# Loading x on one DMA queue, ordering weight loads behind scratch writes, and moving a conversion forward in an engine's order: a Fourier-mixing and MLP kernel on one core

## The chip, the cores and the metric

The kernel runs on one core of one Trainium2 chip. The metric is the device time of one execution in microseconds (us). Each kernel was executed several times, on the same chip as runs of the kernel before, and the medians are given with their range.

The engines go by their names in the profile: PE is TensorE, DVE is VectorE, ACT is ScalarE, POOL is GpSimd, SP is SyncE, and an added q (SPq, POOLq) means the engine's sequencer, which also issues DMAs. In the text I call them TensorE, Vector, Scalar, GpSimd and SyncE.

## The reference

```python
# x: (8, 3008, 256) float32; w_in: (256, 2048) float64; w_out: (2048, 256) float64
X = np.fft.fft(x, axis=1)
X = np.fft.fft(X, axis=2)
x = X.real.astype(np.float32).reshape(24064, 256)
h = x @ w_in
g = h * np.clip(h + 3.0, 0.0, 6.0) / 6.0
return (g @ w_out).astype(np.float32)
```

The weights arrive as 64-bit floats. The kernel computes in float32, so they are loaded in 16 pieces of 512 KB as pairs of 32-bit words and converted to float32 with bit operations. "Conversion" below means this.

## The kernel before

The batches are worked in pairs. For the first pair nothing is there to overlap with, and the kernel begins with a start phase of some 118 us that runs as follows.

1. Eight *chunks* of x are loaded. Each has a direct load (`xt`) and a mirrored one (`xr`), a gather through a list of row numbers `IX`. The two are *folded* (added) on GpSimd, then on Vector.
2. Stage 1 of the Fourier transform multiplies the folded chunk on TensorE. Scalar copies the result out of PSUM as `z`, which I call an *eviction*, and a DMA writes `z` to a scratch in DRAM.
3. When all eight chunks are written, the scratch is read back transposed (`g`), stage 2 runs, and the first matmul of the MLP (`u`) can start.
4. In between, the first weight pieces are converted and folded into the transform (`wps`, `wns`), or mixed (`G`) for w_out.

The order of the program is the order of each engine. That is why it matters where a conversion stands.

```python
def load_x(pr, c):
    xt, xr = x_tile(pr, 2 * c), x_tile(pr, 2 * c + 1)
    nr, eng = (PR + 2, nc.sync) if pr.p == 0 else (PR, nc.gpsimd)    # PR = 94
    rows = x_pn[pr.p * PR:pr.p * PR + nr]
    n = XC if c < NXC - 1 else XC - 1
    eng.dma_start(out=xt[0:nr, 0:n, :], in_=rows[:, c * XC + 1:c * XC + 1 + n, :])
    ...
    nc.gpsimd.indirect_dma_start(                                    # the gather, 94 rows
        out=xr[0:PR].rearrange("p n d -> p (n d)"), out_offset=None, in_=x_r,
        in_offset=bass.IndirectOffsetOnAxis(ap=IX[:, i:i + 1], axis=0))

def stage1(pr, c, i):
    ...
    nc.scalar.copy(z[:, 2 * i:2 * i + 2, :], ps[0:PZ])               # eviction
    if i == XC // 2 - 1:
        (nc.scalar if pr.p == 0 else nc.sync).dma_start(out=..., in_=z[:])   # scratch write

def narrow_a(j):          # Vector: bits; Scalar: three ACTIVATEs for the exponent
    ...
def narrow_b(j):
    st, hi, ex, frac = raw.pop(j)
    nc.vector.scalar_tensor_tensor(ex[:], hi, -2 ** 31, ex[:], op0=AL.bitwise_and, op1=AL.bitwise_or)
    o = st[:].bitcast(F32)[:, 0:WB]
    nc.gpsimd.tensor_tensor(o, frac, ex[:].bitcast(F32), op=AL.mult)
...
load_x(first, 0); load_w(0); load_w(1)
nc.sync.dma_start(out=C[:], in_=...)
load_x(first, 1); load_x(first, 2)
...
narrow_pair(0); use_pair(0)                    # pieces 0 and 1
for c in range(NXC):                           # eight chunks
    fold(first, c, 0, nc.gpsimd)
    fold(first, c, 1, nc.vector)
    if c + 3 < NXC: load_x(first, c + 3)
    if c < 6: load_w(c + 2)
    if c == 5: load_t(0)
    for i in range(XC // 2): stage1(first, c, i)
    if c in (2, 5):                            # pieces 2, 3 (w_in), then 4, 5 (w_out)
        narrow_pair((c + 1) // 3); use_pair((c + 1) // 3)
load_w(8); load_w(9)
load_g(first, 0); load_g(first, 1)             # the read-back
```

## Time and profile before

| | before |
|---|---|
| time, median of 4 (range) | 2093.55 us (2093.17 to 2095.99) |
| span of the profiled execution | 2090.5 us |
| TensorE busy | 1978.4 us, 95% of the span |
| first fold of x starts | 30.55 us |
| last eviction of the start phase ends | 99.65 + 0.58 = 100.23 us |
| read-back issued | 103.39 us |
| stage 2 starts | 108.38 us |
| first `u` matmul starts | 117.73 us |

The last five rows are times in the trace, counted from the start of the span. TensorE is the bound of the whole, but the start phase is a chain of waits. So the first `u` matmul is the mark that I follow. The lines of the profile are in the prediction. There L153 is the first add of a fold, L410 the multiply of a conversion, L195 stage 1, L196 the eviction, L223 stage 2 and L268 the MLP's first layer. The changed kernel is two lines shorter above them, so its numbers are two lower, or one lower from L410 on.

### The profile page before, as it was taken

Reading aid. Unit: us, or ns where it says so; the run is one execution under the profiler, and the core shown is the slowest. Engines: PE = TensorE matmul, PEld = TensorE weight load, DVE = VectorE, ACT = ScalarE, POOL = GpSimd, SP = SyncE. Lnnn points to the kernel's source line nnn. Section 1 sums busy time; section 2 is a strip of 40 time slices with the busy share of each in tenths; the row PEclk is TensorE's granted clock in tenths of the full one; section 3 lists DMA queues with packets and bytes.
Section 4 is the critical chain, followed back from the end, with each engine's and each line's share of the span. In section 5 each row is a group of like instructions: output and inputs, shape, how many; then the busy total and the mean of one; then the engine's idle time right before and its main releaser. Section 6 shows DMA issues by size and latency. Waiting matters only on the chain.

```text
span 2090.5 us, 28142 instructions
## 1 busy us (share of the span) xinstructions
PE 1978.4 (95%) x9136; PEld 1692.8 (81%) x9136; DVE 1455.1 (70%) x2707; ACT 706.7 (34%) x1205; POOL 1499.2 (72%) x1660
## 2 busy tenths in 40 slices
PE   3467999999999999999999999999999999999997
PEld 1246888888888888888888888888888888888886
DVE  4446766777677677767677677677677777777775
ACT  2334333333333333333333333333333333333332
POOL 4437878788677788788667788787866766766765
PEclk7578999999999999999999999999999999999999
DMA  7330221111111112112101111221120011011000
GB/s 200 94 101 21 54 56 42 43 41 45 28 24 31 43 35 60 49 41 50 33 21 32 45 34 43 44 51 48 24 45 11 14 25 21 16 25 21 16 16 18
DMA packets 158272, 86.87 MB, mean 42 GB/s; under 512 B 132496, under 2 KB 145136, under 8 KB 158128
## 3 DMA queue, kind: packets, MB, share of 16 engines
q1 hardware_dynamic: 129968, 60.28, 12.8%
q0 software_dynamic: 27264, 21.65, 3.9%
q10 hardware_dynamic: 896, 3.15, 0.5%
q8 instruction: 74, 1.21, 0.3%
q14 instruction: 70, 0.57, 0.1%
HBM read 47.71 MB, written 37.22 MB: 41 GB/s over the span
## 4 chain that ended last, share of the span: by engine, by line
PE 89%; DVE 3%; ACT 1%; issue 1%; POOL 1%; DMA 0%; SPq 0%; DVEq 0%; POOLq 0%; ACTq 0%
PE acc L322 53%; PE v L268 16%; PE u L268 15%; PE ps L195 2%; PE ps L223 2%; PE ps L239 1%; DVE a L300 1%; ACT t L297 1%; PE wps L447 0%; DVE u L281 0%; DVE s L273 0%; DVE o L348 0%; POOL st L410 0%; DVE v L287 0%; PE ps L192 0%
## 5 line engine op out<-in xcount | busy, mean ns | idle before, releaser
L312 POOL TENSOR_TENSOR c<-a 128x512 f32<-128x512 f32 (+1 forms) x384 | 478.6, 1246 | 408.4 <-DVE a L300 243.2
L322 PE MATMUL acc<-c,G 128*128 128x256 f32 (+1 forms) x3072 | 712.5, 375 | 0.0
L322 PEld LDWEIGHTS acc<-c,G 128*128 128x128 f32 x3072 | 578.5, 190 | 73.3
L297 ACT ACTIVATE t<-u,half 128x512 f32<-128x512 f32 (+2 forms) x416 | 272.2, 654 | 1074.4 <-DVE u L281 1062.8
L273 DVE SCALAR_TENSOR_TENSOR s<-qn,WN,u 128x256 f32<-128x256 f32 x768 | 334.8, 478 | 386.9 <-PE u L268 386.9
L322 PE MATMUL acc<-a,G 128*128 128x256 f32 (+1 forms) x2304 | 554.8, 377 | 0.0
L322 PEld LDWEIGHTS acc<-a,G 128*128 128x128 f32 x2304 | 437.7, 192 | 57.7
L268 PE MATMUL v<-q,W 128*128 128x256 f32 x1536 | 399.3, 383 | 17.9 <-DVE a L300 17.9
L268 PE MATMUL u<-q,W 128*128 128x256 f32 x1536 | 394.5, 379 | 0.0
L268 PEld LDWEIGHTS v<-q,W 128*128 128x128 f32 x1536 | 291.4, 191 | 64.3 <-issue 21.6
L268 PEld LDWEIGHTS u<-q,W 128*128 128x128 f32 x1536 | 287.4, 190 | 65.2 <-issue 20.4
L300 DVE SCALAR_TENSOR_TENSOR a<-t,u 128x512 f32<-128x512 f32 (+2 forms) x416 | 266.2, 646 | 104.8 <-ACT t L297 99.9
L312 POOL TENSOR_TENSOR c<-a,c 128x256 f32<-128x256 f32 (+1 forms) x384 | 274.6, 715 | 30.1
L312 POOL TENSOR_TENSOR c<-c,a 128x256 f32<-128x256 f32 (+1 forms) x384 | 274.5, 715 | 30.1
L281 DVE TENSOR_TENSOR u<-s,v 128x512 f32<-128x512 f32 (+1 forms) x384 | 263.0, 685 | 43.0 <-PE v L268 3.0
L297 ACT ACTIVATE t<-v,half 128x512 f32<-128x512 f32 (+1 forms) x384 | 257.0, 669 | 6.2 <-DVE v L287 4.8
L287 DVE TENSOR_TENSOR v<-v,s 128x512 f32<-128x512 f32 (+1 forms) x384 | 257.9, 672 | 1.1
L300 DVE SCALAR_TENSOR_TENSOR a<-t,v 128x512 f32<-128x512 f32 (+1 forms) x416 | 255.3, 620 | 0.7 <-ACT t L297 0.4
L195 PE MATMUL ps<-y,F 94*96 94x512 f32 x120 | 72.0, 703 | 41.4 <-DVE y L161 35.3
L312 POOL TENSOR_TENSOR r<-w,e 128x256 f32<-128x256 f32 (+1 forms) x96 | 92.2, 981 | 3.8
L328 ACT ACTIVATE e<-acc 128x512 f32<-128x512 f32 (+1 forms) x192 | 86.9, 543 | 2.9 <-PE acc L322 2.8
L348 DVE STREAM_TRANSPOSE o<-r 128x256 f32<-128x256 f32 (+1 forms) x192 | 72.5, 416 | 6.5 <-POOL r L312 6.4
(69 smaller groups left out, 826.4 us busy)
## 6 DMA issues: line engine op xcount, KB each, us to landing
out_dram<-o SPq DMA_DIRECT2D x736, 32.0 KB
g<-zd SPq DMA_DIRECT2D x48, 256.0 KB
zd<-z SPq DMA_DIRECT2D x24, 384.0 KB
xt<-in_x_dram POOLq DMA_DIRECT2D x21, 376.0 KB, 3.9
st<-in_moe_w_in_dram SPq DMA_DIRECT2D x8, 512.0 KB
st<-in_moe_w_out_dram SPq DMA_DIRECT2D x8, 512.0 KB
zd<-z ACTq DMA_DIRECT2D x8, 384.0 KB
xt<-in_x_dram SPq DMA_DIRECT2D x7, 384.0 KB
```

The source lines that it names most:

```text
L195: nc.tensor.matmul(ps[0:PZ], F[0:PR, 0:PZ], y[:, 2 * i:2 * i + 2, :], start=True, stop=True)
L223: nc.tensor.matmul(ps[:, blk, 2 * u:2 * u + 2], g[:, kk, blk * P:(blk + 1) * P], T[:, :, gr, blk, kk], start=True, stop=True)
L268: nc.tensor.matmul(ps[:, i], W1[:, blk, f * P:(f + 1) * P], q[:, blk, of:of + KC], start=True, stop=True)
L273: nc.vector.scalar_tensor_tensor(s[:, i].rearrange("p k n -> p (k n)"), qn[:, of * N2:(of + KC) * N2], WN[:, f:f + 1], u[:, i].rearrange(" ...
L281: nc.vector.tensor_tensor(u[:, :, 0:ns], s[:, :, 0:ns], v[:, :, 0:ns], op=AL.add)
L287: nc.vector.tensor_tensor(v[:, :, 0:nm], v[:, :, 0:nm], s[:, :, 0:nm], op=AL.subtract)
L297: nc.scalar.activation(t, h, AF.Relu, bias=half[:], scale=scale)
L300: nc.vector.scalar_tensor_tensor(dst, t, 1.0, h, op0=AL.min, op1=AL.mult)
L312: nc.gpsimd.tensor_tensor(out, in0, in1, op=AL.add)
L322: nc.tensor.matmul(ch.acc[i // 2][:, i % 2, 0:ch.n], G[:, i, fc, :], mv, start=(fc == 0 and i % 2 == 0), stop=(fc == NF - 1), skip_group_c ...
L328: nc.scalar.mul(ch.e[:, k:i + 1, 0:ch.n], ch.acc[i // 2][:, 0:i + 1 - k, 0:ch.n], 1.0 / WS)
L348: nc.vector.transpose(o[:, 0:n // DH, h], ch.r[:, m, h, 0:n].rearrange("p (j i) -> p j i", i=DH))
```

## The change

Three things are changed in the start phase. All direct loads of x go to GpSimd's queue, with 94 rows instead of 96, so that SyncE's queue has only weights, tables and scratch traffic. Each weight piece from 2 on is issued on SyncE behind a scratch write, which also moves to SyncE, so that pieces no longer crowd the first loads of x: I call this *gating*. And the conversion of pieces 2 to 5 comes ahead of stage 1 of chunks 2 and 5, so ahead of those evictions in Scalar's order, and the multiply of pieces 0 to 5 moves to Vector: I call this *the order*.

```diff
 def load_x(pr, c):
-    nr, eng = (PR + 2, nc.sync) if pr.p == 0 else (PR, nc.gpsimd)
-    rows = x_pn[pr.p * PR:pr.p * PR + nr]
+    rows = x_pn[pr.p * PR:(pr.p + 1) * PR]
-    eng.dma_start(out=xt[0:nr, 0:n, :], in_=...)
+    nc.gpsimd.dma_start(out=xt[:, 0:n, :], in_=...)
 ...
-            (nc.scalar if pr.p == 0 else nc.sync).dma_start(      # scratch write
+            nc.sync.dma_start(
 ...
-        nc.gpsimd.tensor_tensor(o, frac, ex[:].bitcast(F32), op=AL.mult)
+        eng = nc.vector if j < 6 else nc.gpsimd
+        eng.tensor_tensor(o, frac, ex[:].bitcast(F32), op=AL.mult)
 ...
-    load_x(first, 0)
-    load_w(0)
-    load_w(1)
+    for j in range(2):
+        load_w(j)
     nc.sync.dma_start(out=C[:], ...)
-    load_x(first, 1)
-    load_x(first, 2)
+    for c in range(3):
+        load_x(first, c)
 ...
     for c in range(NXC):
 ...
-        if c < 6:
-            load_w(c + 2)
-        if c == 5:
-            load_t(0)
+        if c in (2, 5):
+            narrow_pair((c + 1) // 3)
         for i in range(XC // 2):
             stage1(first, c, i)
+        for j in {0: (2, 3), 2: (4,), 3: (5,), 5: (6,), 6: (7,), 7: (8, 9)}.get(c, ()):
+            load_w(j)
+        if c == 4:
+            load_t(0)
         if c in (2, 5):
-            narrow_pair((c + 1) // 3)
             use_pair((c + 1) // 3)
-    load_w(8)
-    load_w(9)
     load_g(first, 0)
```

(The tile of x shrinks to 94 rows, and a memset moves from GpSimd to Vector.)

## The prediction

> **What bounds the kernel now.** I read the page first, for where TensorE is not yet full. Its 40 slices are 52 us each:
>
> ```profile
> PE   3467999999999999999999999999999999999997
> PEclk7578999999999999999999999999999999999999
> ...
> PE 89%; DVE 3%; ACT 1%; issue 1%; POOL 1%; DMA 0%; SPq 0%; DVEq 0%; POOLq 0%; ACTq 0%
> ```
>
> From the fifth slice on (about 200 us) TensorE is at 90% or more, and the chain that ended last is 89% TensorE. The change touches nothing there. What it can win lies in the first four slices. The stretches of 20 us (columns: stretch, length, busy us with instruction counts for PE, PEld, DVE, ACT, POOL; granted clock, DMA share, GB/s) say how they are filled:
>
> ```profile
> 20.00:40.00 20.00, 6.79 (x24) 3.22 (x22) 3.02 (x6) 2.20 (x5) 7.99 (x6) 0.65 0.73 183
> 80.00:100.00 20.00, 7.96 (x16) 3.92 (x16) 8.71 (x19) 4.89 (x10) 9.81 (x10) 0.50 0.16 47
> ...
> 180.00:200.00 20.00, 14.61 (x63) 12.33 (x62) 13.39 (x23) 8.65 (x15) 15.05 (x18) 0.83 0.00 1
> 200.00:220.00 20.00, 20.00 (x91) 16.80 (x89) 15.04 (x28) 7.73 (x14) 16.75 (x19) 1.00 0.18 39
> ```
>
> No engine is full before 200 us: this is a chain of waits. So I followed it in order of time (start, length, engine, line, what; in brackets the idle time before it and what ended it):
>
> ```profile
> 4.03 1.70 POOL L141 DMA_INDIRECT xt<-in_x_dram,IX  x1 [3.58 <-DVE IX L465]
> 30.55 1.25 POOL L153 TENSOR_TENSOR xt<-xt 94x508 f32<-94x508 f32 x1 [12.83 <-DMA xt<-in_x_dram,IX]
> 51.08 0.72 ACT L398 ACTIVATE ex<-ex,bias 128x512 f32<-128x512 int32 x1 [0.44 <-ACT z L196]
> 54.12 1.27 POOL L410 TENSOR_TENSOR st<-top,ex 128x512 f32<-128x512 f32 x1 [9.34 <-DVE ex L408]
> 80.00 1.26 POOL L410 TENSOR_TENSOR st<-top,ex 128x512 f32<-128x512 f32 x1 [11.39 <-DVE ex L408]
> 86.36 1.26 POOL L153 TENSOR_TENSOR xt<-xt 94x508 f32<-94x508 f32 x1
> 108.38 3.52 PE L223 MATMUL ps<-T,g 128*128 128x128 f32 x16 [8.76 <-DMA g<-zd]
> 117.73 1.11 PE L268 MATMUL u<-q,W 128*128 128x256 f32 x4
> ```
>
> Three waits stand out. The first fold of x starts at 30.55 us, 24.8 us after its gather was issued (4.03 + 1.70 = 5.73). Later GpSimd, which folds in order, twice sits idle (9.34 and 11.39 us) in front of a multiply of the weight conversion, because Scalar reaches the conversion only after the evictions z. And all eight chunks must be stored to the scratch and read back (108.38) before the first MLP matmul at 117.73 us, which I take as the mark of the start: what it gains, the whole gains.
>
> Why the gather takes 25 us the DMA view of the first 40 us and the page's issue list tell:
>
> ```profile
> q1 hardware_dynamic: 2630, 7.20, 66.5%
> q0 software_dynamic: 3005, 1.28, 16.0%
> ...
> xt<-in_x_dram,IX POOLq DMA_INDIRECT x5, 26.4
> ```
>
> ```profile
> xt<-in_x_dram POOLq DMA_DIRECT2D x21, 376.0 KB, 3.9
> ...
> xt<-in_x_dram,IX POOLq DMA_INDIRECT x32, 12.6
> ```
>
> A direct load on GpSimd's queue lands in 3.9 us, a gather over the whole run in 12.6, in the first 40 us in 26.4 (medians). The trace's packet records say more. In mid-run a gather's 94 rows of 4096 B pass at 81 packets from 217 to 224 us, about 12 per us at 0.159 us each: two DMA engines' worth. From 10 to 20 us, 616 packets of the software queue stand beside 622 of SyncE's queue, so they alternate; 576 of the 616 are of 4 B and only 40 are rows. SyncE had a backlog of F 192, C 257, seven xt of 384 and five pieces of 512: 5,697 KB.
>
> **What the Trainium skill says.** "DMA: Bandwidth & Descriptors", section "Queues, rings and completion order": each DMA engine round-robins between queues packet by packet; 616 against 622 agrees. Same page, "Why a DMA increments its semaphore by 16 and not by 1": the engines used are the largest number up to 16 that divides the outer sizes, with an exception for some direct copies from GpSimd. 94 gives 2 for the gather, and the direct load gets nearly all; 12.6 against 3.9 us agrees. So padding x to 96 rows was for SyncE's queue, and dropping it on GpSimd's costs nothing. "GPSIMD Engine Reference", section "4.1 Engine selection": GpSimd is about twice as slow on two-input elementwise work. The multiply takes 1.26 us there; Vector's two-input add of the same 128x512 takes 0.69.
>
> **The change part by part.** All start times of the changed kernel are estimates from durations above and from before's trace.
>
> 1. x leaves SyncE. Ahead of the first scratch write SyncE has only F, two pieces and C: 192 + 1024 + 257 = 1,473 KB, at before's roughly 300 GB/s about 5 us, gone by 8 us. The gather of chunk 0 is issued at about 4.1 to 5.8 (it still needs IX from F), then takes as in mid-run, where from issue end to the fold 10.6 us (214.6 to 225.2) and 11.6 us passed. First fold at about 17: 13.5 us earlier. The cost: eight direct issues of 0.6 us plus gaps of 0.3 on GpSimd, so the period of a fold and its loads grows from 4.4 to 5.4 us (2.35 fold, 0.9 direct, 2.1 gather). Chunk 3's gather is issued only after fold 0, and lands 11 to 14 us later with the weights and scratch writes in between: some 37. So x itself sets 6 to 7 us a chunk.
>
> 2. The conversions of pieces 2 to 5 come before stage 1 of chunks 2 and 5 in Scalar's order, and their multiply goes to Vector. This takes 4 x 1.26 = 5.0 us off GpSimd and its two long idle times, 9.34 + 11.39 = 20.7 us, out of the fold chain. Fold 3 no longer waits for a conversion. But pieces 2 and 3 follow the first scratch write: fold 0 at 17 + 2.4 fold + 1.5 Vector + 4.3 for stage 1 at the half clock and evictions = 25.7, landed by 32. Conversion from 32 to 38.3 (Scalar six ACTIVATEs, 4.5 us, plus Vector), matmuls wps and wns until 44.5, stage 1 of chunk 3 behind them in TensorE's order; fold 3 (38.4) was ready. Fold 4 at 42, fold 5 at 47.5, fold on Vector done 51.4. Piece 5 follows the fourth scratch write, landing at 51, about on time. Conversion to 57.8, then GpSimd's mixing of w_out to 60.8, then fold 6. In before, fold 6 (86.36) to the last eviction (100.23) took 13.9 us; so the last eviction comes at 74.7. If the gathers suffer more from scratch writes and pieces (28 packets per DMA engine between chunks 0 and 2, at 0.25 us each instead of half of that), 78. I take 76 against 100.2: 24 us earlier.
>
> 3. From there nothing changes in kind: scratch write, read-back, stage 2, wps, first MLP matmul took 17.5 us. Pieces 8 and 9 (1 MB, 3 us) now lie ahead of the read-back on SyncE, mostly under the 3.1 us in which the last write lands anyway; I add 1 us. First MLP matmul at 76 + 17.5 + 1 = 94.5 against 117.7.
>
> 4. Moving the memset of ones (0.23 us) and the scratch writes from Scalar's to SyncE's queue: nothing on the path.
>
> After it the ramp to 200 us (pieces 8 to 15 converted beside the MLP) and the MLP itself keep order and length. Sum: 2093.2 - 23.2 = 2070.
>
> **The rivals.**
> - *The two-engine gathers become the bound.* Three gathers in flight share rings with direct loads behind them; GpSimd does nothing else to hide them. For it: 12.6 us each even alone, 26.4 in a crowd. Against: different gathers seem to run on different engine pairs (20 rows per us around 26 us). At 8 us a chunk the last eviction comes near 88: 2082.
> - *The weight pieces become the wait.* Each is behind a scratch write, piece 5 lands when it is needed, piece 7 the same. If each pair costs 3 us more: 2077.
> - *The start was hidden anyway*, because weight conversions set the pace until 200 us. Against: conversion of piece 8 starts at 126 us, after the first MLP matmuls in Vector's order, so it moves with them. It would leave 2093; I give it little.
> - *More than I think*: TensorE idle less, so at the higher clock (0.50 in 80 to 100 us), and fold 6 sooner: 2060. A floor: eight folds and loads at 5.4 us from 17 us, 3 us of mixing and the tail of 12 give about 75; so 2% (42 us) is out of reach.
>
> **Range and chances.** Errors in the gathers' landing add up over three generations of chunks, mostly to the late side; the early side is closed by GpSimd's own work. Predicted 2070, 8 in 10 from 2060 to 2084. Faster by over 2% (under 2051): 0.03; within 2%: 0.95; slower by over 2%: 0.02.
>
> **What would show it.** First fold near 17 us instead of 30.55; GpSimd's idle times before folds ended by gathers and no longer by conversions; the last z eviction near 76; the first u matmul near 94.5, and a constant shift from there to the end. Wrong if the first fold stays past 25, if GpSimd waits over 8 us a chunk for gathers, if Vector or TensorE waits for pieces 5 or 7, or if the shift at the first u matmul does not arrive at the end.

## The result, and the profile after

| | before | after | predicted for after |
|---|---|---|---|
| time, median of 4 (range) | 2093.55 (2093.17 to 2095.99) | 2080.44 (2079.59 to 2080.97) | 2070, 2060 to 2084 |
| first fold | 30.55 | 18.27 | 17 |
| stage 1 of chunk 3 starts | 63.41 | 54.99 | 44.5 |
| fold 6 starts | 86.36 | 70.83 | 60.8 |
| last eviction ends | 100.23 | 84.70 | 76 |
| first `u` matmul | 117.73 | 105.66 | 94.5 |
| span of the profile | 2090.5 | 2078.6 | |

The ratio of after to before is 0.9935, with a 95% interval from 0.9917 to 0.9952. Here and below, a ratio is the mean time of one kernel's fast runs over that of the other's in the same rounds, so it is not quite the ratio of the medians. The verdict is "same", inside 2%, as the chances had it, and the time is inside the range. But the gain is 2093.55 - 2080.44 = 13.1 us where 23.2 was predicted.

The gain arrives whole. The mark moved by 117.73 - 105.66 = 12.1 us and the end of the profiled span by 2090.5 - 2078.6 = 11.9 us. So nothing was given back later, and the missing ten microseconds must be found before 105.66 us. The slices of the page after, and its chain by engine, show the same in coarse form:

```profile
PE   4468999999999999999999999999999999999997
PEclk7688999999999999999999999999999999999999
...
PE 91%; DVE 4%; DMA 2%; ACT 1%; issue 1%; POOL 1%; SPq 0%; DVEq 0%; POOLq 0%; ACTq 0%
```

Only the first slices differ from before. In the chain DMA has grown from 0% to 2%: waits for data that were not on the chain before are on it now. The stretches of 20 us (the columns are as in the prediction) say where DMAs are busy:

```profile
20.00:40.00 20.00, 11.39 (x29) 4.25 (x27) 6.49 (x15) 5.38 (x10) 12.62 (x12) 0.63 0.69 189
...
80.00:100.00 20.00, 8.64 (x30) 6.49 (x29) 3.33 (x6) 6.89 (x11) 3.57 (x3) 0.50 0.80 211
```

From 80 to 100 us the DMA share went from 0.16 to 0.80: the read-back and pieces 8 and 9 now share this stretch. In order of time, the first 60 us of the kernel after are these (start, length, engine, line, what; in brackets the idle time before it and what ended it):

```profile
18.27 1.26 POOL L151 TENSOR_TENSOR xt<-xt 94x508 f32<-94x508 f32 x1 [8.06 <-DMA xt<-in_x_dram,IX]
...
25.02 1.20 SPq L378 DMA_DIRECT2D st<-in_moe_w_in_dram  x2
...
36.56 0.43 DVE L395 TENSOR_SCALAR ex<-st 128x512 int32<-128x512 int32 x1 [4.51 <-DMA st<-in_moe_w_in_dram]
...
39.40 0.43 DVE L395 TENSOR_SCALAR ex<-st 128x512 int32<-128x512 int32 x1 [1.02 <-DMA st<-in_moe_w_in_dram]
...
42.00 1.05 ACT L194 COPY z<-ps 96x512 f32<-96x512 f32 x2
...
44.30 3.63 DVE L406 SCALAR_TENSOR_TENSOR ex<-st,ex 128x512 int32<-128x512 int32 x1
...
45.07 1.27 POOL L151 TENSOR_TENSOR xt<-xt 94x508 f32<-94x508 f32 x1
...
57.57 0.30 SPq L196 DMA_DIRECT2D zd<-z  x1
...
57.99 0.40 SPq L381 DMA_DIRECT2D st<-in_moe_w_out_dram  x1
```

The reader should see four things. The first fold is at 18.27 us, nearly where it was expected. Pieces 2 and 3 are issued at 25.02 us behind the first scratch write, but Vector can begin on them only at 36.56 and 39.40 us, and both waits are ended by the piece's own DMA. The evictions of chunk 2, now behind the conversion in Scalar's order, wait until 42.00 us, although their stage-1 matmuls had ended by 35.9. And the fourth scratch write comes only at 57.57 us, so piece 5, which is behind it, leaves at 57.99. The rest of the start phase:

```profile
63.62 0.43 DVE L395 TENSOR_SCALAR ex<-st 128x512 int32<-128x512 int32 x1 [3.50 <-DMA st<-in_moe_w_out_dram]
...
66.86 1.11 POOL L433 TENSOR_TENSOR G<-st 128x256 f32<-128x256 f32 x1 [13.85 <-DVE st L409]
...
70.83 1.25 POOL L151 TENSOR_TENSOR xt<-xt 94x508 f32<-94x508 f32 x1
...
84.12 0.58 ACT L194 COPY z<-ps 96x512 f32<-96x512 f32 x1 [1.93 <-PE ps L190]
...
95.44 3.75 PE L221 MATMUL ps<-T,g 128*128 128x128 f32 x16 [11.36 <-DMA g<-zd]
...
105.66 1.11 PE L266 MATMUL u<-q,W 128*128 128x256 f32 x4
```

Piece 5 lands at 63.62 us, and GpSimd, which should be folding chunk 6, stands idle for 13.85 us until it may mix the converted w_out. The idle times of 9.34 and 11.39 us that the change was to remove are gone, and one of 13.85 us stands in their place.

### The profile page after: what moved, and what is told of

It is laid out like the page before. It is cut to its first block, busy times and chain, and to the rows that moved or that the text cites. A ratio compares the mean times of both kernels' runs of the same rounds, so it can differ in the third digit from the quotient of the medians.

```text
span 2078.6 us, 28133 instructions
## 1 busy us (share of the span) xinstructions
PE 1974.6 (95%) x9136; PEld 1692.0 (81%) x9136; DVE 1456.9 (70%) x2714; ACT 706.1 (34%) x1205; POOL 1496.1 (72%) x1662
## 2 busy tenths in 40 slices
DMA packets 158161, 86.81 MB, mean 42 GB/s; under 512 B 132512, under 2 KB 145056, under 8 KB 158016
## 4 chain that ended last, share of the span: by engine, by line
PE 91%; DVE 4%; DMA 2%; ACT 1%; issue 1%; POOL 1%; SPq 0%; DVEq 0%; POOLq 0%; ACTq 0%
PE acc L320 53%; PE v L266 16%; PE u L266 15%; PE ps L193 2%; PE ps L221 2%; PE wps L446 1%; PE ps L237 1%; DVE a L298 1%; DMA st<-in_moe_w_in_dram 1%; ACT t L295 1%; DVE u L279 0%; DVE ex L406 0%; DVE s L271 0%; PE wns L451 0%; DMA g<-zd 0%
## 5 line engine op out<-in xcount | busy, mean ns | idle before, releaser
L193 PE MATMUL ps<-y,F 94*96 94x512 f32 x120 | 67.0, 656 | 26.2 <-DVE y L159 20.1
```

The source lines that it names most:

```text
L193: nc.tensor.matmul(ps[0:PZ], F[0:PR, 0:PZ], y[:, 2 * i:2 * i + 2, :], start=True, stop=True)
```

## The experiments

My theory after reading this was: *x on GpSimd's queue and the order each do what was expected of them, and the gating takes a good part of it back, because a piece that starts late behind a scratch write also lands late beside the gathers.* The rivals were that the two-engine gathers set the pace, that the multiply on Vector costs more than it saves, and that the read-back behind pieces 8 and 9 is what is missing. Twelve kernels were run, five rounds each. All gave correct results. The kernel before took 2093.89, 2093.34 and 2093.65 us. The kernel after was not run again, so a comparison with it goes over the kernel before. The two columns of marks come from one profiled execution each: the kernel after, g_first and piece5 are the same program up to the first fold and have it at 18.27, 19.00 and 19.90 us, so a difference of under 2 us between two marks proves little.

| kernel | first fold | first `u` | time, median | ratio to before [95%] |
|---|---|---|---|---|
| before | 30.55 | 117.73 | 2093.55 | 1 |
| after | 18.27 | 105.66 | 2080.44 | 0.9935 [0.9917, 0.9952] |
| x_only | 22.72 | 107.57 | 2083.75 | 0.9952 [0.9938, 0.9965] |
| order_only | 32.08 | 109.45 | 2083.98 | 0.9950 [0.9936, 0.9963] |
| gate_only | 24.07 | 119.00 | 2093.71 | 1.0002 [0.9989, 1.0016] |
| x_order | 22.37 | 95.02 | 2071.90 | 0.9895 [0.9880, 0.9911] |
| x_gate | 19.66 | 108.70 | 2082.66 | 0.9946 [0.9932, 0.9960] |
| mult_pool | 18.14 | 108.28 | 2083.67 | 0.9955 [0.9942, 0.9969] |
| g_first | 19.00 | 104.56 | 2079.79 | 0.9924 [0.9911, 0.9938] |
| pieces23 | 21.61 | 106.50 | 2080.88 | 0.9935 [0.9922, 0.9947] |
| piece5 | 19.90 | 102.54 | 2075.31 | 0.9907 [0.9892, 0.9922] |
| gather96 | 13.03 | 99.19 | 2076.00 | 0.9916 [0.9903, 0.9930] |
| x_order_g96 | 13.42 | 90.86 | 2066.34 | 0.9869 [0.9854, 0.9885] |
| late_mix | 13.47 | 82.11 | 2062.42 | 0.9840 [0.9826, 0.9853] |

### x_only: the kernel before with x on GpSimd's queue

```diff
-        return pool.tile([PR + 2, XC, D], F32, tag=tag, name="xt")
+        return pool.tile([PR, XC, D], F32, tag=tag, name="xt")
-        nr, eng = (PR + 2, nc.sync) if pr.p == 0 else (PR, nc.gpsimd)
+        nr, eng = PR, nc.gpsimd
```

Expected:

> The kernel before with one part of the change: all of x on GpSimd's queue. Theory (the changed kernel's start is bound by the loop scratch write, weight piece, conversion, eviction, next scratch write; the gain comes from the earlier first fold): SyncE now has 3,009 KB of F, C and five pieces unhindered by x, so the first gather lands at 20 to 23 us instead of 30.55; pieces are early, but the two idle times of GpSimd before conversions (9.3 and 11.4 us) stay. First u matmul near 109, time 2083 to 2087. Rival (x on GpSimd gives the whole gain, order and gating are worth nothing): first u matmul at 105.7 as in the changed kernel, 2080.

Measured: the first fold came at 22.72 us, the first `u` at 107.57, the time was 2083.75 us (2081.94 to 2085.11). GpSimd's timeline of this kernel:

```profile
44.44 1.27 POOL L410 TENSOR_TENSOR st<-top,ex 128x512 f32<-128x512 f32 x1 [6.64 <-DVE ex L408]
...
69.66 1.27 POOL L410 TENSOR_TENSOR st<-top,ex 128x512 f32<-128x512 f32 x1 [9.34 <-DVE ex L408]
```

One part alone gives three quarters of the gain of the whole change. The two idle times before the multiplies are still there, as they must be without the order.

### order_only: the kernel before with the conversions moved

```diff
+        if c in (2, 5):
+            narrow_pair((c + 1) // 3)
         for i in range(XC // 2):
             stage1(first, c, i)
         if c in (2, 5):
-            narrow_pair((c + 1) // 3)
             use_pair((c + 1) // 3)
...
-        nc.gpsimd.tensor_tensor(o, frac, ...)
+        eng = nc.vector if j < 6 else nc.gpsimd
+        eng.tensor_tensor(o, frac, ...)
```

Expected:

> The kernel before with the conversions of pieces 2 to 5 ahead of stage 1 of chunks 2 and 5 in Scalar's order and their multiply on Vector. Theory: first fold stays at 30.5, the idle times of GpSimd before conversions go, since the pieces are there early: first u matmul 8 to 12 us earlier (106 to 110), time 2082 to 2086. Rival (the chunks are bound by the gathers, so order only uncovers a wait for x): under 4 us, 2089 to 2093.

Measured: first fold 32.08 us, first `u` 109.45, time 2083.98 us (2082.74 to 2085.16). This part alone also gives about 10 us, although x is as late as before. GpSimd's waits did not all go, as I had expected: it still stood idle for 12.67 us until it could mix the converted w_out.

### gate_only: the kernel before with pieces behind scratch writes

```diff
-            (nc.scalar if pr.p == 0 else nc.sync).dma_start(
+            nc.sync.dma_start(
...
-        if c < 6:
-            load_w(c + 2)
-        if c == 5:
-            load_t(0)
         for i in range(XC // 2):
             stage1(first, c, i)
+        for j in {0: (2, 3), 2: (4,), 3: (5,), 5: (6,), 6: (7,), 7: (8, 9)}.get(c, ()):
+            load_w(j)
+        if c == 4:
+            load_t(0)
...
-    load_w(8)
-    load_w(9)
```

Expected:

> The kernel before with the scratch writes on SyncE and each piece behind one, x on SyncE as before. Theory: the backlog ahead of the first gather falls from 5,697 to about 3,000 KB, first fold at 20 to 23 us, but pieces 2 to 5 come late, and x of later chunks on SyncE now also stands behind scratch writes: first u matmul 112 to 120, time 2086 to 2096. Rival (gating alone is the cure of the starved gather): first u matmul near 105, 2081.

Measured: first fold 24.07 us, first `u` 119.00, time 2093.71 us (2092.95 to 2097.42), a ratio of 1.0002. GpSimd's timeline:

```profile
24.07 1.25 POOL L153 TENSOR_TENSOR xt<-xt 94x508 f32<-94x508 f32 x1 [6.73 <-DMA xt<-in_x_dram,IX]
...
53.10 1.26 POOL L410 TENSOR_TENSOR st<-top,ex 128x512 f32<-128x512 f32 x1 [15.80 <-DVE ex L408]
```

The first fold is 6.5 us sooner, because the pieces no longer crowd it, and the wait before the multiply of the conversion is 15.80 us instead of 9.34: 6.46 us longer. The gating hands x its time and takes it from the weights. At the last eviction (98.74 us) the kernel is still 1.5 us ahead of the kernel before; from there to the first `u` it takes 20.26 us instead of 17.50, which Step 3 below explains.

### x_order and x_gate: the two missing corners

x_order is the kernel before with the edits of x_only and of order_only and no gating. x_gate is the kernel after without the order:

```diff
-        eng = nc.vector if j < 6 else nc.gpsimd
-        eng.tensor_tensor(o, frac, ex[:].bitcast(F32), op=AL.mult)
+        nc.gpsimd.tensor_tensor(o, frac, ex[:].bitcast(F32), op=AL.mult)
...
-        if c in (2, 5):
-            narrow_pair((c + 1) // 3)
         for i in range(XC // 2):
             stage1(first, c, i)
...
         if c in (2, 5):
+            narrow_pair((c + 1) // 3)
             use_pair((c + 1) // 3)
```

Expected of x_order:

> The change without the gating: x on GpSimd's queue, conversions ahead of the evictions and their multiply on Vector, but pieces and scratch writes queued as in the kernel before. The single parts moved the first u matmul by -10.2 (x_only), -8.3 (order_only) and +1.3 us (gate_only); their sum is -17, the whole change has only -12.1. Theory (gating is what costs, through the loop scratch write, piece, conversion, eviction): first fold at 22 to 23, later than in the changed kernel, but no wait for pieces 2 to 5; first u matmul 98 to 101, time 2073 to 2077, faster than the changed kernel. Rival (x and order win the same time, both being bound by the gathers, and gating is harmless): 104 to 107, 2079 to 2083.

Expected of x_gate:

> The change without the order: x on GpSimd's queue and the gating, but conversions behind the evictions and their multiply on GpSimd, as in the kernel before. Theory (gating delays the pieces, so conversions wait for pieces and what order could win is partly lost): first u matmul 108 to 113, time 2083 to 2089, that is x_only (107.6, 2083.75) or worse. Rival (gating helps x, which order does not need): 104 to 106, 2080.

Measured: x_order had its first `u` at 95.02 us and took 2071.90 us (2070.05 to 2072.58). x_gate had it at 108.70 and took 2082.66 us (2081.85 to 2084.11). With x on GpSimd's queue in all four, the first `u` is:

| | without the order | with the order | the order is worth |
|---|---|---|---|
| without gating | 107.57 (x_only) | 95.02 (x_order) | 12.6 |
| with gating | 108.70 (x_gate) | 105.66 (after) | 3.0 |
| the gating costs | 1.1 | 10.6 | |

This is the central reading. The gating does little harm as long as the conversion is late anyway. It does harm once the order puts the conversion early and it waits there for its pieces. The times say the same: with the order the gating costs 2080.44 - 2071.90 = 8.5 us, and without it nothing that can be measured (2082.66 against 2083.75).

The cost can be split where the last eviction ends, at 89.89 us in x_only, 76.75 in x_order, 88.87 in x_gate and 84.70 in the kernel after. Of the 10.6 us, 8.0 arise before it, in the chain of pieces and conversions, and 2.7 behind it, in the read-back. Without the order the chain is 1.0 us shorter with gating and the read-back 2.2 us longer. GpSimd's timeline of x_order shows both sides of the trade:

```profile
22.37 1.25 POOL L153 TENSOR_TENSOR xt<-xt 94x508 f32<-94x508 f32 x1 [10.50 <-DMA xt<-in_x_dram,IX]
...
59.72 0.74 POOL L435 TENSOR_TENSOR G<-st 128x256 f32<-128x256 f32 x1 [6.51 <-DVE st L411]
```

Against the kernel after, the first fold is 4.1 us later, and yet the mixing of w_out starts 7.1 us sooner (59.72 against 66.86) after an idle time of 6.51 us instead of 13.85. x_order came out better than I had expected. It gains 117.73 - 95.02 = 22.7 us at the mark where the two parts alone gain 10.2 and 8.3. I have no run that explains the 4 us by which the two together exceed their sum.

### mult_pool: the kernel after with the multiply back on GpSimd

```diff
-        eng = nc.vector if j < 6 else nc.gpsimd
-        eng.tensor_tensor(o, frac, ex[:].bitcast(F32), op=AL.mult)
+        nc.gpsimd.tensor_tensor(o, frac, ex[:].bitcast(F32), op=AL.mult)
```

Expected:

> The changed kernel with the multiply of pieces 0 to 5 back on GpSimd. Theory (conversion is bound by the pieces' landing, so which engine multiplies matters little; but GpSimd's in-order multiply stands ahead of folds 3 and 4): each pair 1 to 2 us later, first u matmul 106 to 110, 2081 to 2085. Rival (the multiply on Vector collides with GpSimd's adds, as the 3.6 us beside one of 0.7 suggest, and costs more than it saves): first u matmul 101 to 104, 2076 to 2079.

Measured: first `u` at 108.28 us, time 2083.67 us (2083.20 to 2085.97). So the multiply on Vector saves 2.6 us at the mark and 3.2 in the time; the rival that it costs more than it saves is out.

### g_first: the kernel after with pieces 8 and 9 behind the first half of the read-back

```diff
-        for j in {..., 6: (7,), 7: (8, 9)}.get(c, ()):
+        for j in {..., 6: (7,)}.get(c, ()):
             load_w(j)
...
     load_g(first, 0)
+    load_w(8)
+    load_w(9)
     load_g(first, 1)
```

Expected:

> The changed kernel with the read-back of group 0 issued ahead of pieces 8 and 9, which follow it, and group 1 after them. Theory (the 7.6 us of the read-back, against 5.0 in the kernel before, come from the 1 MB ahead of it on SyncE's queue): the read-back lands about 2.5 us sooner after the last scratch write, first u matmul near 103, time 2077 to 2079. Rival (the read-back is slow for another reason): first u matmul unchanged at 105.7, 2080.

Measured: stage 2 starts 93.94 - 85.78 = 8.2 us after the issue of the last scratch write, against 95.44 - 84.72 = 10.7 in the kernel after. So the two pieces in front cost the read-back 2.5 us. The last write itself was 1.1 us later in this profile. The time was 2079.79 us (2075.91 to 2080.84), which overlaps the range of the kernel after: whether these 2.5 us arrive at the end is not settled by this run.

### pieces23 and piece5: gating taken off single pieces of the kernel after

```diff
 pieces23:
-    for j in range(2):
+    for j in range(4):
         load_w(j)
...
-        for j in {0: (2, 3), 2: (4,), 3: (5,), ...
+        for j in {2: (4,), 3: (5,), ...
 piece5:
-        for j in {0: (2, 3), 2: (4,), 3: (5,), 5: (6,), ...
+        for j in {0: (2, 3), 1: (4,), 2: (5,), 5: (6,), ...
```

Expected of pieces23:

> The changed kernel with pieces 2 and 3 sent ahead of the first scratch write, behind C; the other pieces gated as in the change. Theory (two turns of the loop cost: pieces 2 and 3 behind write 0, piece 5 behind write 3; each 3 to 5 us): first fold later, at 20 to 23 us, since 1 MB more stands beside the first gather, but wps of the second pair at 43 instead of 44.5 with its second half at once, stage 1 of chunk 3 at 51 instead of 55; first u matmul 100 to 103, time 2075 to 2078. Rival (the later first fold takes back what the early pieces give): 105 to 107, 2080 to 2082.

Expected of piece5:

> The changed kernel with pieces 4 and 5 each one scratch write earlier (behind writes 1 and 2). Theory: piece 5 is issued near 43 instead of 58 us and is there when Vector reaches it at 58 to 59 us, so fold 6 comes 4 to 5 us earlier (66 instead of 70.8); first u matmul 100.5 to 102.5, time 2075 to 2077. Rival (more traffic beside the gathers of chunks 4 and 5 delays folds 4 and 5 by as much): 105, 2080.

Measured: pieces23 gave 2080.88 us (2079.37 to 2082.99), no better than the kernel after, and here the rival was right. Its first fold is 3.3 us later (21.61), its stage 1 of chunk 3 is 4.9 us sooner (50.06), and then piece 5 eats the gain. SyncE's timeline of pieces23:

```profile
53.05 0.39 SPq L381 DMA_DIRECT2D st<-in_moe_w_out_dram  x1
```

and Vector's:

```profile
63.75 0.43 DVE L395 TENSOR_SCALAR ex<-st 128x512 int32<-128x512 int32 x1 [6.60 <-DMA st<-in_moe_w_out_dram]
```

Piece 5 is issued 4.9 us sooner than in the kernel after, and lands at the same time (63.75 against 63.62). It now takes 10.7 us instead of 5.6, in a stretch in which the gathers of chunks 6 and 7 are in flight until about 64 us.

piece5 gave 2075.31 us (2073.10 to 2077.35), 5 us less than the kernel after. There the piece was issued at 45.70 us, and the mixing began at 63.40 instead of 66.86. At the mark this is 3.1 us. So each of the two ties delays the chain, but to free the first pair alone gains nothing while piece 5 stays tied: it has to leave early enough, and not just earlier.

### gather96 and x_order_g96: the gathers over 96 rows

The list of rows is extended to 96 (the two further rows fetch row 0 and are not used):

```diff
-    IX = consts.tile([PR, NP * NXC], I32, name="IX")
+    IX = consts.tile([PR + 2, NP * NXC], I32, name="IX")
-        return pool.tile([PR, XC, D], F32, tag=tag, name="xt")
+        return pool.tile([PR + 2, XC, D], F32, tag=tag, name="xt")
-        nc.gpsimd.dma_start(out=xt[:, 0:n, :], in_=...)
+        nc.gpsimd.dma_start(out=xt[0:PR, 0:n, :], in_=...)
-    nc.vector.tensor_copy(IX[:], F[0:PR, 5 * PZ:])
+    nc.vector.tensor_copy(IX[:], F[:, 5 * PZ:])
```

gather96 is this edit on the kernel after. x_order_g96 is the same idea on x_order.

Expected of gather96:

> The changed kernel with the gathers over 96 rows instead of 94 (two rows more, of index 0, unused), so that 16 divides the rows. If the number of rows sets how many DMA engines a gather uses, it lands in about 4 us instead of 12 to 16. Theory (pieces land in 11 to 14 us because they share engines packet by packet with the two-engine gathers): first fold near 10 to 11 us, pieces 2 and 3 land within 5 us of their issue, first u matmul 85 to 92, time 2060 to 2068. Rival (the pieces are late only because they stand behind scratch writes): only the first fold's 7 us come, first u matmul near 98, 2073. If the row count does not matter: 2080.

Expected of x_order_g96:

> The same with gathers over 96 rows. Theory: first fold at 12 to 16 us, no chunk waits for x and none for a piece until piece 5 or 6; first u matmul 85 to 92, time 2061 to 2069. Rival (Vector and Scalar work and TensorE's order of conversion matmuls and stage 1 bound the start once x is there): no better than 95, 2071.

The view of the DMAs by kind over the whole run (out and in, queue, operation, number of them, then median us from issue to landing) says for the kernel after:

```profile
xt<-in_x_dram,IX POOLq DMA_INDIRECT x32, 12.5
```

and for gather96:

```profile
xt<-in_x_dram,IX POOLq DMA_INDIRECT x32, 4.9
```

Two more rows make the gather 2.5 times as fast. Measured: gather96 took 2076.00 us (2073.94 to 2077.58), with the first fold at 13.03 us and the first `u` at 99.19. That is a gain over the kernel after of 4.4 us, less than my theory had expected and nearer to the rival's figure. GpSimd's timeline of gather96 says why:

```profile
13.03 1.68 POOL L151 TENSOR_TENSOR xt<-xt 94x508 f32<-94x508 f32 x1 [4.57 <-DMA xt<-in_x_dram,IX]
...
60.39 1.11 POOL L433 TENSOR_TENSOR G<-st 128x256 f32<-128x256 f32 x1 [22.32 <-DVE st L409]
```

x is early by 5 us, and GpSimd then waits 22.32 us for the converted w_out. The gathers were not the bound; the gated pieces still were. Pieces 2 and 3, issued at 27.66 us, were there for Vector at 33.82 and 37.86, after 6.2 and 10.2 us instead of 11.5 and 14.4. So, as far as one profile of each tells, the 94 rows have a share of some 4 to 5 us in their late landing. But they did not land within 5 us, as my theory had it, and what holds them up beyond that stays open.

The first scratch write was even issued 2.6 us later than in the kernel after (27.28 against 24.64). Vector's last two instructions on piece 0 begin at the same time in both kernels (13.51 and 13.54 us). In gather96, where GpSimd is folding chunk 0 then (13.03 to 16.20), they took 1.75 and 1.46 us; in the kernel after, where GpSimd is idle then, 0.68 and 0.69. TensorE's matmuls on pieces 0 and 1, which stand ahead of stage 1, so began at 16.80 us instead of 15.01.

The edit changes one thing more. The packets under 512 B fall from 132,512 in the kernel after to 111,456, so a gather over 94 rows brings 658 small packets (4 B in the records) that one over 96 does not. 658 is 14 x 47, as if two engines carried 47 rows each and each of the other fourteen got 47 such packets. The records name no engine, so this is an inference. No run separates the two-engine rows from these packets as the cause of the crowd.

x_order_g96 took 2066.34 us (2065.66 to 2067.39), first `u` at 90.86, as expected.

### late_mix: x_order_g96 with w_out's first pair after the read-back

In x_order_g96 GpSimd still waits before the mixing (16.53 us), with the folds of chunks 6 and 7 behind it. But `G` is needed only by the second layer of the MLP. So the pair leaves the start phase:

```diff
-        if c in (2, 5):
-            narrow_pair((c + 1) // 3)
+        if c == 2:
+            narrow_pair(1)
         for i in range(XC // 2):
             stage1(first, c, i)
-        if c in (2, 5):
-            use_pair((c + 1) // 3)
-    load_w(8)
-    load_w(9)
+        if c == 2:
+            use_pair(1)
     load_g(first, 0)
     load_g(first, 1)
     load_t(1)
+    load_w(8)
     narrow_pair(3)
 ...
     use_pair(3)
+    narrow_pair(2)
+    use_pair(2)
+    load_w(9)
```

Expected:

> An attempt to beat all: x_order_g96 with the conversion and mixing of pieces 4 and 5 (w_out, not needed before mlp2) taken out of the fold chain, behind the conversion of pieces 6 and 7; pieces 8 and 9 behind the read-back. In x_order_g96 GpSimd waits 17.6 us (37.5 to 55.1) for that conversion ahead of folds 6 and 7. Theory: folds 6 and 7 follow at 39 to 43 us, the last eviction comes 12 to 15 us earlier, 3 to 5 us come back as conversion before the first MLP step and as the late piece 9: first u matmul 78 to 84, time 2055 to 2063. Rival (the conversion only moves to a place where mlp2 waits for it): mark earlier, but the end at 2064 to 2070.

Measured: 2062.42 us (2056.38 to 2064.41), 1.6% faster than the kernel before and the best of all. TensorE's timeline:

```profile
82.11 1.11 PE L268 MATMUL u<-q,W 128*128 128x256 f32 x4
```

The mark is 117.73 - 82.11 = 35.6 us sooner, the time 31.2 us lower (2093.65 - 2062.42). The profiled execution is the slowest of the five, and its span is 2090.5 - 2062.6 = 27.9 us shorter. So some 4 to 8 us are given back after the mark, where the moved pair now stands. This run also moves pieces 8 and 9 behind the read-back, so its gain is that of both edits.

## Why the prediction was right or wrong

**Step 1, x leaves SyncE: right.** "First fold at about 17" came at 18.27 us. The gain at this point is 12.3 us where 13.5 was forecast. The claim that dropping the padding costs nothing was right of the direct loads (3.9 us median in both). That 94 gives the gather only two engines, which the prediction took from the Trainium skill's page "DMA: Bandwidth & Descriptors", section "Why a DMA increments its semaphore by 16 and not by 1", agrees with gather96: 96 is divisible by 16, and the landing falls from 12.5 to 4.9 us. Beside the weights the gathers were slower than forecast: chunk 3's was issued by 23.28 us and its fold started at 39.78, 16.5 us later, where 11 to 14 were expected.

**Step 2, conversions ahead of the evictions: the mechanism was right, a term was mis-sized.** The term is "Pieces 2 and 3 follow the first scratch write: ... landed by 32", and with it "Piece 5 follows the fourth scratch write, landing at 51, about on time". The issue of pieces 2 and 3 was right to 0.7 us (25.7 predicted, 25.02 measured), in part by luck: the prediction's terms add up to 25.2 and not 25.7, the first fold was 1.3 us late, and the way from there to the first scratch write took 6.4 us instead of 8.2. Their landing was not: 36.56 and 39.40 us, 11.5 and 14.4 us after the issue, where I had allowed some 6. That is little more than an uncrowded landing: in the kernel after the median for such a piece over the run is 4.4 us. The packet records show a long tail. Of the 352 packets of 4096 B of the first scratch write and the two pieces, some 315 have started by 32.5 us. Then the second scratch write joins them, and from 37 to 41 us the last packets of SyncE's queue pass at 13, 7, 7 and 2 per us, beside 25 to 33 rows of x per us. I read this so: a piece has landed only when its last share has, and that share stands on an engine which a two-engine gather is filling. The records do not tell which engine a packet used. gather96 suggests that the 94 rows are worth some 4 to 5 us of these landings, and not the whole. The skill's same page, section "Issuing engines are not separate DMA queues", says that all DMAs run on the same 16 engines and interleave, whoever issued them; these records agree. Separate queues did not keep x and the weights apart.

What followed was a chain of the size of that error:

- The conversion was done at 48.66 us instead of 38.3. Of the 10.4 us, 7.4 are the second piece's landing (39.40 against 32). Most of the remaining 3 are one Vector instruction, L406, which took 3.63 us from 44.30 where it took 0.68 on piece 2. It ended at 47.93, just after GpSimd's two adds of fold 4 (45.07 to 47.38). The skill's page "SBUF — State Buffer", section "Who interferes with whom", says that a Vector instruction with two inputs in SBUF contends with a GpSimd instruction that reads SBUF. This instruction has two such inputs, and the trace agrees. No run isolates it here, but gather96 shows such a case: Vector's last two instructions on piece 0 took 1.75 and 1.46 us beside a fold and 0.68 and 0.69 without one.
- Stage 1 of chunk 3 started at 54.99 us instead of 44.5, so the fourth scratch write left at 57.57. Piece 5 was tied to that write and landed at 63.62 instead of 51. The lateness of one pair thus became the lateness of the next. In Vector's order the two can be told apart: its fold of chunk 5 was done at 58.40 us instead of 51.4, which is the first pair's 7.0 us, and then it waited 3.50 us for piece 5. That is the property of the gating which I had not worked out: it makes the weights wait for the chain, while the order makes the chain wait for the weights.
- The mixing began at 66.86 us instead of 57.8, and fold 6 at 70.83 instead of 60.8.
- From fold 6 to the end of the last eviction 13.9 us were predicted, and 84.70 - 70.83 = 13.87 were measured. So the last eviction was late by 84.70 - 76 = 8.7 us. It is less than the 10 us of fold 6, because I had moved the estimate from 74.7 to 76 for slow gathers.

That the gating is the cause is shown by x_order: without it the first `u` comes at 95.02 us and the time is 2071.90, and Vector waits for none of pieces 2 to 5. That these figures are nearly the 94.5 and 2070 which I predicted for the changed kernel is in part chance, since x_order's first fold is 5 us later than the 17 predicted.

**Step 3, "From there nothing changes in kind ... I add 1 us": right in kind, too small.** From the end of the last eviction to the first `u` it took 105.66 - 84.70 = 20.96 us, against 17.5 in the kernel before. So 3.5 us were added, and not 1. The read-back, from its issue to stage 2, took 95.44 - 87.79 = 7.65 us instead of 108.38 - 103.39 = 4.99, as 1 MB of pieces 8 and 9 stands in front of it. SyncE's timeline of the kernel before has:

```profile
103.39 2.61 SPq L208 DMA_DIRECT2D g<-zd  x4
```

and that of the kernel after:

```profile
85.13 1.13 SPq L378 DMA_DIRECT2D st<-in_moe_w_in_dram  x2
87.79 2.61 SPq L206 DMA_DIRECT2D g<-zd  x4
```

g_first shows that this is their doing: with the read-back's first half ahead of them, 2.5 us come back at stage 2. The other runs bear it out. From the last eviction to the first `u` it takes 19.8 to 21.7 us in the seven kernels that issue pieces 8 and 9 behind the last scratch write and ahead of the read-back, 17.5 to 18.3 in the five that have them early, and 18.8 in g_first.

**Step 4, a memset and the scratch writes move, "nothing on the path": not tried alone.** The move of the scratch writes is part of gate_only, whose ratio is 1.0002; but on SyncE's queue they are what ties the pieces to the chain.

**The sum.** 8.7 us at the last eviction and 2.5 us in the read-back make 11.2 us, which is the distance from 94.5 to 105.66. At the end the gain was 10.1 us short (23.2 against 13.1), within the scatter of the runs.

**The rivals.** "The weight pieces become the wait" is what happened, with the size mis-judged: I had given it 3 us a pair. "The two-engine gathers become the bound" was wrong as stated, since gather96 removes them and GpSimd then waits for w_out instead; but they have a share in the pieces' late landing, as gather96 shows. "The start was hidden anyway" was wrong: the shift at the mark arrived at the end in full. "More than I think" did not come either: from 80 to 100 us the granted clock is 0.50 in both kernels.

**The signs.** One of the prediction's own signs of being wrong came true: Vector waited for pieces 5 and 7 (3.50 us, and 6.04 us until 85.55). And of what would show it right, two signs failed: GpSimd's longest idle time, the 13.85 us ahead of the mixing and fold 6, is still ended by a conversion, and the last eviction is at 84.70. That the time lies within 2060 to 2084 is due to the width of the range on its late side.

## What to carry to other kernels

When a load is tied behind a step of the same chain that later waits for it, count its landing from the latest moment that step can happen, and with the transfers that will be in flight then, not from an uncrowded case. Before tying loads to one another to keep them out of each other's way, look at what makes the crowd: here in part gathers over 94 rows, which 96 rows made 2.5 times as fast (worth 2071.90 - 2066.34 = 5.6 us without the gating). And work that nothing in the start phase needs, such as w_out's mixing, should stand behind the chain and not in it: taking it out, with pieces 8 and 9 moved behind the read-back, was worth another 8.8 us at the mark (90.86 - 82.11) and 3.9 us in the time.

## What the Trainium skill lacked or had wrong

- "DMA: Bandwidth & Descriptors", section "Why a DMA increments its semaphore by 16 and not by 1": it makes an exception for some direct copies from GpSimd, and does not say whether gathers fall under it. Here they do not: 94 rows took a median of 12.5 us, 96 rows 4.9, while direct loads of 94 rows on the same queue took 3.9.
- The same page has nothing on what a transfer over all engines costs when a gather over 94 rows is in flight beside it. Two pieces of 512 KB, with a median of 4.4 us over the run, took 11.5 and 14.4 us beside such gathers in the kernel after, and 6.2 and 10.2 us beside gathers over 96 rows.
- The same page does not tell of the small packets that a gather brings when 16 does not divide its rows: 658 more per gather over 94 rows than over 96 (132,512 packets under 512 B against 111,456, for 32 gathers). In the kernel before, some 580 of the 620 packets of GpSimd's queue from 10 to 20 us were of 4 B, beside about as many packets of SyncE's queue; that these small ones count as turns between the queues fits this, but is not shown.
